# Row maxima transposed before they are clamped, bucket rows scaled on ACT, low parts subtracted on Pool

## The chip, the cores and the metric

The kernel runs on one core of a Trainium2 chip. The metric is the device time of one execution in microseconds (us). The engines are named as in the profile: PE (TensorE; PEld is its weight load), DVE (VectorE), ACT (ScalarE), POOL (GpSimd), SP (SyncE, which only issues transfers here). "SPq" and "ACTq" are the transfer queues of SP and ACT.

## The reference

Attention with buckets, and then a feed-forward net with a rational activation. There are 4 batches, 8 heads, 768 positions and 64 channels a head.

```python
q_bits = (np.einsum('bhsd,dk->bhsk', q, proj) > 0)          # 6 bits: the bucket of a position
mask = q_bucket[:, :, :, None] == k_bucket[:, :, None, :]
scores = np.where(mask, scale * (q @ k.T), -1e9)
scores = scores - np.max(scores, axis=-1, keepdims=True)
attn = np.exp(scores)
attn = attn / (np.sum(attn, axis=-1, keepdims=True) + 1e-09)
x = attn @ v                                                # -> 3072 tokens x 512
h = x @ w_in                                                # 512 x 2048
P = a0 + a1*h + a2*h**2 + a3*h**3
Q = 1 + |b0|*|h| + |b1|*h**2
out = (P / (Q + 1e-6)) @ w_out                              # 2048 x 512
```

## The kernel before

Two heads form a pair p, and there are 16 pairs. All large products run with float32 operands split in a rounded high part (fp32r) and the rest, the low part. For each pair:

- `high` rounds q and k on ACT into Q1 and K1 (tiles of 3 buffers); `high_move` brings half of them to the other partitions with two transfers; `low` subtracts the high part from the raw operand (DVE) into LO, of which there is one buffer for q and one for k; `second_low` and `second_high` send LO and Q1/K1 to Q2 and K2.
- `bits`, once for two pairs, projects q and k on 6 directions (PE, tile psb in PSUM), and DVE compares them with zero and subtracts a constant of the partition (tile mb); a second DVE operation multiplies each row by a factor of its partition, 2^60 or 1. `maskrows` moves the rows to rows 64 and up of Q1 and K1, so that a product over 76 rows gives the score plus a term of that size where bits differ.
- `maxstep(p, j)`, 12 times a pair, forms scores for 128 queries and 768 keys (PE, tile psm, two buffers) and reduces them to a column of M with a maximum (DVE).
- `shift_clamp` turns M (128 x 12) into nm = -max(M, -2^40) on DVE, SBUF to SBUF; `shift_turn` transposes nm on PE into PSUM (tile pst, one of the three "s" buffers, which scores use too) and copies it to mt on ACT; `shift_rows` moves mt to row 76 of Q1, where it shifts the scores.
- `scores(p, s)`, 12 steps a pair: the products pss on PE with keys on the partitions, exp on ACT into one of six E tiles, and additions of E tiles (acc, POOL), 8 a pair.
- `values` multiplies E with V (psv), `sums` adds up acc over the keys (psu), `values_out` and `sums_store` send both to DRAM; `recips` forms reciprocals on DVE once for 4 pairs.

`weights(i)`, 32 pieces spread over the attention, splits w_in and w_out in high and low parts (ACT, DVE): its DVE operations appear as wr, ws, wi_lo in the profile.

The order is written out by hand. `at(p, s, f, ...)` puts a step at place 12 p + s of a plan, sorted at the end; steps of the same place keep the order in which they were added. Each engine runs its instructions strictly in that program order (`Ordered`). Work for pair p is put two pairs ahead (`high`, `low`, `bits`, `maskrows`, `maxstep` from place 7 on) or one pair ahead (`second_low`, `second_high`, `load_v`, the shift steps at places 7, 8 and 10). Nearly all transfers are issued by SP. For pair 0 the shift is done in two halves of the queries (hf = 0, 1), and the steps ahead of the plan are written in line; the low parts of pair 1 are subtracted on Pool there.

The feed-forward net (`Ffn`, `Gemm1`: psh, pso, gl, c, w in the profile) follows, with PE as its busiest engine.

All instructions carry the line of the helper that issues them, L61; so groups are told apart by the names of tiles.

Of the kernel before, what the change touches and what calls it, by code (L numbers as in the profile page):

```python
# [7 lines left out]
F32 = mybir.dt.float32  # L8
# [3 lines left out]
AF = mybir.ActivationFunctionType  # L12
ALU = mybir.AluOpType
# [4 lines left out]
P = 128  # L18
S = 768
HQ = 384  # L20
NT = S // P
# [13 lines left out]
CLAMP = 2.0 ** 40  # L35
# [30 lines left out]
def move(nc, out, in_, queue=None):  # L66

    (queue or nc.sync).dma_start(out.bitcast(F32), in_.bitcast(F32))
# [3 lines left out]
def bucket_attention_then_rational_ffn(ctx, tc, qT, kT, v, proj, w_in, w_out, coef, consts, out):  # L72
# [55 lines left out]
    def operands_to_terms():  # L128
        early.close()
        ffn.terms_pool(right)  # L130

    last = attention(tc, nc, raw, ps_b, tail, tokens, early, operands_to_terms, ffn, load, QF, KF, v, w_in, w_out, wo_d, ident, cst,
                     ones, prj, wi_hi, wi_lo, x_d, s_d, r_d, coefficients)
    ffn.rest(ctx, last)
# [3 lines left out]
def attention(ctx, tc, nc, raw, ps_b, tail, tokens, early, operands_to_terms, ffn, load, QF, KF, v, w_in, w_out, wo_d, ident, cst, ones, prj,  # L138
# [9 lines left out]
    sm = ctx.enter_context(tc.tile_pool(name="sm", bufs=1))  # L148
# [5 lines left out]
    Q1, Q2, K1, K2, LO, V, M, MB, ACC, EXP, AV, MS = ({} for _ in range(12))  # L154

    def load_v(p, queue=nc.sync):
        V[p] = operand("v", p, [P, NT, P], F32)
        queue.dma_start(V[p], v[p])
# [3 lines left out]
    def high(p, t):  # L162
        F, T, n = ((QF, Q1, "q"), (KF, K1, "k"))[t]
        T[p] = operand(f"{n}1", p, [P, 2, S], F32R, 3)
        nc.scalar.copy(T[p][:, t, :], F[p])

    def high_move(p):
        for T, g in ((Q1[p], 0), (K1[p], 1)):
            move(nc, T[0:64, 1 - g, :], T[64:128, g, :])

    def low(p, t, engine=nc.vector):
        F, T = ((QF, Q1), (KF, K1))[t]
        LO[p, t] = raw.tile([P, S], F32R, tag=f"lo{t}", name=f"lo{t}_{p}", bufs=1)
        engine.tensor_tensor(out=LO[p, t], in0=F[p], in1=T[p][:, t, :].bitcast(F32), op=ALU.subtract)
# [13 lines left out]
    def bits(p, which=(0, 1)):  # L188

        if which[0] == 0:  # L190
            mb = sm.tile([P, 2, HQ], F32R, tag="mb", name=f"mb{p}")
            MB[p], MB[p + 1] = (mb, 0), (mb, 64)
        mb = MB[p + which[0]][0]
        sl = slice(64 * which[0], 64 * which[-1] + 64)
        ps = ps_a.tile([P, 2, 512], F32, tag="psa", name=f"psb{p}_{which[0]}")
        for hf in range(2):
            for w in which:
                for t, F in enumerate((QF[p + w], KF[p + w])):
                    o = 64 * w + 32 * t
                    nc.tensor.matmul(ps[o : o + 32, hf, 0:HQ], prj[:, t, :], F[:, hf * HQ : hf * HQ + HQ], start=True, stop=True)  # L200
        rows = mb[sl]
        nc.vector.tensor_scalar(out=rows, in0=ps[sl, :, 0:HQ], scalar1=0.0, scalar2=cst[sl, 0:1], op0=ALU.is_gt, op1=ALU.subtract)
        nc.vector.tensor_scalar(out=rows, in0=rows.bitcast(F32), scalar1=cst[sl, 1:2], scalar2=None, op0=ALU.mult)

    def maskrows(p, queues=(None, None)):
        mb, o = MB.pop(p)
        for h in range(2):
            o1 = o + 14 * h
            move(nc, Q1[p][64:76, h, :], mb[o1 : o1 + 12].rearrange("p f c -> p (f c)"), queues[0])
            move(nc, K1[p][64:77, h, :], mb[o1 + 32 : o1 + 45].rearrange("p f c -> p (f c)"), queues[1])  # L210
# [9 lines left out]
        nc.vector.tensor_reduce(out=M[p][:, j : j + 1], in_=ps[:, :, 0:HQ], axis=AX.XY, op=ALU.max)  # L220


    def shift_clamp(p, hf=None):
        m = M[p].rearrange("p (h f i) -> p h f i", h=2, f=2)
        m = m if hf is None else m[:, :, hf : hf + 1, :]
        n = NT if hf is not None else 2 * NT
        MS[p] = sm.tile([P, n], F32, tag="nm", name=f"nm{p}_{hf}")
        nc.vector.tensor_scalar(out=MS[p].rearrange("p (h f i) -> p h f i", h=2, i=NT // 2), in0=m, scalar1=-CLAMP, scalar2=-1.0,
                                op0=ALU.max, op1=ALU.mult)

    def shift_turn(p, hf=None):
        n = NT if hf is not None else 2 * NT
        ps = ps_b.tile([P, 512], F32, tag="s", bufs=3, name=f"pst{p}_{hf}")
        nc.tensor.transpose(ps[0:n, 0:P], MS.pop(p), ident)
        MS[p] = sm.tile([n, P], F32R, tag="mt", name=f"mt{p}_{hf}")
        nc.scalar.copy(MS[p], ps[0:n, 0:P])

    def shift_rows(p, hf=None):
        cs = slice(0, S) if hf is None else slice(hf * HQ, hf * HQ + HQ)
# [62 lines left out]
    def recips(bb):  # L302
        n = 2 * NHP * S // P
        s = tail.tile([P, n], F32, tag="rs", name=f"rs{bb}")
        nc.sync.dma_start(s, s_d[bb].rearrange("h (x c) -> (h x) c", c=n))
        yield
        z = tail.tile([P, n], F32, tag="rz", name=f"rz{bb}")
        d = tail.tile([P, n], F32, tag="rd", name=f"rd{bb}")
        r = tail.tile([P, n], F32, tag="rr", name=f"rr{bb}")
        nc.vector.tensor_scalar(out=z, in0=s, scalar1=0.0, scalar2=S * TINY, op0=ALU.is_equal, op1=ALU.mult)  # L310
        nc.vector.tensor_scalar(out=d, in0=s, scalar1=0.0, scalar2=1e-9, op0=ALU.is_gt, op1=ALU.mult)
        nc.vector.tensor_tensor(out=d, in0=s, in1=d, op=ALU.add)
        nc.vector.tensor_tensor(out=d, in0=d, in1=z, op=ALU.add)
        nc.vector.reciprocal(out=r, in_=d)
        yield
        nc.sync.dma_start(r_d[bb].rearrange("h (x c) -> (h x) c", c=n), r)
        yield
# [43 lines left out]
    def at(p, s, f, *args):  # L361
        plan.setdefault(12 * p + s, []).append((f, args))

    def spread(p, steps, gen):
        for s in steps:
            at(p, s, lambda g: next(g, None), gen)

    for p in range(NPAIR):
        for s in range(12):
            at(p, s, scores, p, s)  # L370

            if p > 1:
                at(p - 2, 7 + s if p > 2 else 9 + 0.85 * s, maxstep, p, s)

            if not 0 < p < NPAIR - 1:
                at(p, s + 2.3, values, p, s)
            elif s % 2:
                at(p, s + 1.3, values, p, s - 1)
                at(p, s + 1.3, values, p, s)
            if s % NT == NT - 1:  # L380
                at(p, s + (1.3 if 0 < p < NPAIR - 1 else 2.3), values_out, p, s // NT)
        for hf in range(2):
            at(p, 6 * hf + 9, values_store, p, hf)
        if p < NPAIR - 1:
            at(p, 14.5, sums, p)
            at(p, 16, sums_store, p)
        if p > 1:
            for t in range(2):
                at(p - 2, t, high, p, t)
                at(p - 2, 2 + t, low, p, t)  # L390
            if p % 2 == 0:
                at(p - 2, 3 if p == 2 else 2, bits, p)
            at(p - 2, 2, high_move, p)
            at(p - 2, 6 if p == 2 else 4, maskrows, p)
        if p > 0:
            at(p - 1, 0, second_low, p)
            at(p - 1, 3, second_high, p)
            at(p - 1, 4, load_v, p)
            d = 1.5 if p == 1 else 0
            at(p - 1, 7 + d, shift_clamp, p)  # L400
            at(p - 1, 8 + d, shift_turn, p)
            at(p - 1, 10 if d == 0 else 9.6, shift_rows, p)
        if p > 3:
            at(p - 4, 6, load, p)
        if p % NHP == NHP - 1 and p + 1 < NPAIR:
            spread(p, (20, 22, 23), recips(p // NHP))
# [12 lines left out]
    for t in range(2):  # L419
        high(0, t)  # L420
        low(0, t)
    bits(0, (0,))
    high_move(0)
    maskrows(0, (nc.sync, nc.scalar))
    load(2, nc.scalar)
    load_v(0, nc.scalar)
    bits(0, (1,))
    for t in range(2):
        high(1, t)
    second_low(0)  # L430
# [5 lines left out]
        at(-2, when[s], maxstep, 0, order[s])  # L436
        at(0, 0.6 + 0.7 * s, maxstep, 1, s)
    for hf in range(2):
        for s, f in ((5, shift_clamp), (6.5, shift_turn), (6.6, shift_rows)):
            at(-2, 19.5 * hf + s, f, 0, hf)  # L440
    for t in range(2):
        low(1, t, nc.gpsimd)
# [211 lines left out]
```

## Time and profile before

| | |
|---|---|
| median of 3 runs | 1029.55 us (1029.2 to 1035.9) |
| profiled execution | 1029.27 us, of which the span is 1027.5 us |
| busy PE | 977.0 us, 95% of the span |
| busy DVE | 907.9 us, 88% |
| busy ACT | 678.9 us, 66% |
| busy POOL | 384.8 us, 37% |
| transfers | 112.95 MB, mean 110 GB/s |

A row of a group reads: line, engine, operation, out<-in, shapes, count | busy us, mean ns of one | idle time of the engine just before, and what ended it. A row of waits reads: who waited <- for whom: us in total, times, longest. A row of the timeline reads: start us, length us, engine, operation, and in brackets the idle time before it and its releaser. The chain is the work that ended last, followed back from the end. A row of stretches gives the length and the busy time (instructions) of PE, PEld, DVE, ACT and POOL, the clock that PE was granted (1.00 is full speed), the busy share of the transfer engines and GB/s. A row of one tile gives min/median/max in ns.

### The profile page before, as it was taken

The page shows a single profiled execution, that of the slowest core. Times are in us where ns is not written, and L with a number is a line of the kernel's source. Part 1 is how long each engine was busy: PE and PEld are TensorE (multiplying, and loading weights), DVE is VectorE, ACT ScalarE, POOL GpSimd, SP SyncE. Part 2 cuts the span into 40 slices and gives each one's busy share as a digit, 9 for nine tenths or more (in the row PEclk, how much of TensorE's full clock was granted, in tenths as well). Part 3 has the DMA queues.
Part 4 walks back from the last instruction along what each step waited for, and adds up shares of the span by engine and source line. Part 5 has one row for each costly group of instructions (what it writes and reads, how often), then busy time and mean ns, then how long its engine had stood idle before and what let it go on. Part 6 is the DMA issues. An engine that isn't in the chain of part 4 may idle for free.

```text
span 1027.5 us, 14486 instructions
## 1 busy us (share of the span) xinstructions
PE 977.0 (95%) x5009; PEld 749.4 (73%) x5009; DVE 907.9 (88%) x1207; ACT 678.9 (66%) x1419; POOL 384.8 (37%) x268
## 2 busy tenths in 40 slices
PE   6899988989898988999999999999999999999998
PEld 2565555555555555564999999999999999999996
DVE  5688788878978787767999999999999999999996
ACT  1466555656656655567877777777777777777775
POOL 1255554545545454556222222222222222222222
PEclk7799999999999999899999999999999999999999
DMA  7765564656656664673740201101111010020000
GB/s 202 195 165 175 165 177 124 177 163 186 187 165 211 206 205 134 177 217 118 283 137 15 69 11 62 32 1 62 32 57 36 1 62 31 1 72 22 32 1 31
DMA packets 50489, 112.95 MB, mean 110 GB/s; under 512 B 9296, under 2 KB 21968, under 8 KB 50416
## 3 DMA queue, kind: packets, MB, share of 16 engines
q1 hardware_dynamic: 49580, 110.59, 35.8%
q10 hardware_dynamic: 836, 1.44, 0.5%
q8 instruction: 39, 0.64, 0.3%
q14 instruction: 34, 0.28, 0.1%
HBM read 56.82 MB, written 21.17 MB: 76 GB/s over the span
## 4 chain that ended last, share of the span: by engine, by line
PE 78%; DVE 13%; DMA 3%; issue 2%; ACT 2%; SPq 1%; DVEq 0%; ACTq 0%
PE psh L61 26%; PE pso L61 26%; PE psv L61 10%; PE pss L61 9%; PE psm L61 4%; DVE m L61 3%; DVE wr L61 2%; DVE ws L61 2%; DVE nm_None L61 2%; PE psu L61 2%; DVE wi_lo L61 2%; ACT E L61 1%; DMA k<-k 1%; PE psb L61 1%; SPq L61 1%
## 5 line engine op out<-in xcount | busy, mean ns | idle before, releaser
L61 POOL TENSOR_TENSOR gl<-c,gh 128x384 fp32r<-128x384 f32 x128 | 140.6, 1099 | 396.0 <-ACT gh L61 369.4
L61 DVE TENSOR_REDUCE m<-psm 128x1 f32<-128x768 f32 x192 | 180.1, 949 | 76.8 <-PE psm L61 76.2
L61 PE MATMUL pso<-wo,gh 128*128 128x512 f32 x768 | 241.1, 395 | 0.0
L61 ACT ACTIVATE E<-pss 128x384 f32<-128x384 f32 x384 | 168.4, 490 | 97.9 <-PE pss L61 92.4
L61 POOL TENSOR_TENSOR acc<-E,E 128x768 f32<-128x768 f32 x64 | 126.2, 1972 | 190.3 <-ACT E L61 190.3
L61 PE MATMUL pss<-q,k 77*128 77x384 f32 (+1 forms) x768 | 183.1, 361 | 3.0 <-DMA q<-mt 2.6
L61 PEld LDWEIGHTS pss<-q,k 77*128 77x128 f32 (+1 forms) x768 | 136.7, 196 | 64.6 <-issue 54.4
L61 PE MATMUL psh<-xl,wi_hi 128*128 128x384 f32 x512 | 172.1, 336 | 0.0
L61 PE MATMUL psh<-xh,wi_hi 128*128 128x384 f32 x512 | 171.7, 335 | 0.0
L61 PE MATMUL psh<-xh,wi_lo 128*128 128x384 f32 x512 | 171.5, 335 | 0.0
L61 PEld LDWEIGHTS pso<-wo,gh 128*128 128x128 f32 x768 | 142.9, 188 | 23.7
L61 PE MATMUL psv<-E,v 128*64 128x385 f32 x768 | 157.3, 529 | 0.0
L61 PE MATMUL pso<-wo,gl 128*128 128x512 f32 x384 | 152.2, 396 | 0.3 <-POOL gl L61 0.3
L61 DVE SCALAR_TENSOR_TENSOR c<-c,ab,r 128x384 f32<-128x384 f32 x128 | 147.1, 1149 | 0.0
L61 ACT ACTIVATE h<-psh 128x384 f32<-128x384 f32 x128 | 63.1, 493 | 122.4 <-PE psh L61 122.4
L61 POOL TENSOR_TENSOR acc<-acc,E 128x768 f32<-128x768 f32 x64 | 113.9, 1780 | 30.1 <-ACT E L61 27.5
L61 PE MATMUL psm<-k,q 76*128 76x384 f32 x384 | 111.1, 374 | 13.9 <-DVE m L61 9.8
L61 PEld LDWEIGHTS psh<-xh,wi_hi 128*128 128x128 f32 x512 | 96.1, 188 | 6.3 <-issue 1.2
L61 PEld LDWEIGHTS psh<-xl,wi_hi 128*128 128x128 f32 x512 | 96.0, 188 | 5.1
L61 PEld LDWEIGHTS psh<-xh,wi_lo 128*128 128x128 f32 x512 | 96.1, 188 | 0.0
L61 PEld LDWEIGHTS psm<-k,q 76*128 76x128 f32 x384 | 71.7, 204 | 31.8 <-DVE m L61 22.2
L61 PEld LDWEIGHTS psv<-E,v 128*64 128x64 f32 x768 | 47.6, 141 | 64.1 <-issue 56.7
(63 smaller groups left out, 1322.6 us busy)
## 6 DMA issues: line engine op xcount, KB each, us to landing
q<-q SPq DMA_DIRECT2D x48, 192.0 KB
k<-k SPq DMA_DIRECT2D x48, 192.0 KB
wr<-w_in SPq DMA_DIRECT2D x16, 512.0 KB
wr<-w_out SPq DMA_DIRECT2D x16, 512.0 KB
wo_d<-wr SPq DMA_DIRECT2D x16, 512.0 KB
wo<-wo_d SPq DMA_DIRECT2D x16, 512.0 KB
q<-lo SPq DMA_DIRECT2D x32, 192.0 KB
k<-lo SPq DMA_DIRECT2D x32, 192.0 KB
```

Source lines behind the costliest of these rows:

```text
L61: return self.tc.keep_in_program_order(issue(*args, **kwargs))
```

## The change

- `shift_clamp` is gone. `shift_turn` transposes M itself, and DVE clamps the result as it copies it out of PSUM to mt; ACT's copy is gone. For the two halves of pair 0 a DVE copy gathers the half's columns first.
- The scaling of the bucket rows becomes a step of its own, `penalties`, on ACT, one place behind `bits`.
- `low` runs on Pool for pairs 2 to 15.

```diff
--- before.py
+++ after.py
@@ -198,9 +198,12 @@
                 for t, F in enumerate((QF[p + w], KF[p + w])):
                     o = 64 * w + 32 * t
                     nc.tensor.matmul(ps[o : o + 32, hf, 0:HQ], prj[:, t, :], F[:, hf * HQ : hf * HQ + HQ], start=True, stop=True)
-        rows = mb[sl]
-        nc.vector.tensor_scalar(out=rows, in0=ps[sl, :, 0:HQ], scalar1=0.0, scalar2=cst[sl, 0:1], op0=ALU.is_gt, op1=ALU.subtract)
-        nc.vector.tensor_scalar(out=rows, in0=rows.bitcast(F32), scalar1=cst[sl, 1:2], scalar2=None, op0=ALU.mult)
+        nc.vector.tensor_scalar(out=mb[sl], in0=ps[sl, :, 0:HQ], scalar1=0.0, scalar2=cst[sl, 0:1], op0=ALU.is_gt, op1=ALU.subtract)
+
+    def penalties(p, which=(0, 1)):
+        sl = slice(64 * which[0], 64 * which[-1] + 64)
+        rows = MB[p + which[0]][0][sl]
+        nc.scalar.activation(rows, rows.bitcast(F32), AF.Identity, scale=cst[sl, 1:2])
 
     def maskrows(p, queues=(None, None)):
         mb, o = MB.pop(p)
@@ -220,20 +223,15 @@
         nc.vector.tensor_reduce(out=M[p][:, j : j + 1], in_=ps[:, :, 0:HQ], axis=AX.XY, op=ALU.max)
 
 
-    def shift_clamp(p, hf=None):
-        m = M[p].rearrange("p (h f i) -> p h f i", h=2, f=2)
-        m = m if hf is None else m[:, :, hf : hf + 1, :]
-        n = NT if hf is not None else 2 * NT
-        MS[p] = sm.tile([P, n], F32, tag="nm", name=f"nm{p}_{hf}")
-        nc.vector.tensor_scalar(out=MS[p].rearrange("p (h f i) -> p h f i", h=2, i=NT // 2), in0=m, scalar1=-CLAMP, scalar2=-1.0,
-                                op0=ALU.max, op1=ALU.mult)
-
     def shift_turn(p, hf=None):
-        n = NT if hf is not None else 2 * NT
+        n, m = 2 * NT, M[p]
+        if hf is not None:
+            n, m = NT, sm.tile([P, NT], F32, tag="nm", name=f"nm{p}_{hf}")
+            nc.vector.tensor_copy(m.rearrange("p (h i) -> p h i", h=2), M[p].rearrange("p (h f i) -> p h f i", h=2, f=2)[:, :, hf, :])
         ps = ps_b.tile([P, 512], F32, tag="s", bufs=3, name=f"pst{p}_{hf}")
-        nc.tensor.transpose(ps[0:n, 0:P], MS.pop(p), ident)
+        nc.tensor.transpose(ps[0:n, 0:P], m, ident)
         MS[p] = sm.tile([n, P], F32R, tag="mt", name=f"mt{p}_{hf}")
-        nc.scalar.copy(MS[p], ps[0:n, 0:P])
+        nc.vector.tensor_scalar(out=MS[p], in0=ps[0:n, 0:P], scalar1=-CLAMP, scalar2=-1.0, op0=ALU.max, op1=ALU.mult)
 
     def shift_rows(p, hf=None):
         cs = slice(0, S) if hf is None else slice(hf * HQ, hf * HQ + HQ)
@@ -387,9 +385,10 @@
         if p > 1:
             for t in range(2):
                 at(p - 2, t, high, p, t)
-                at(p - 2, 2 + t, low, p, t)
+                at(p - 2, 2 + t, low, p, t, nc.gpsimd)
             if p % 2 == 0:
                 at(p - 2, 3 if p == 2 else 2, bits, p)
+                at(p - 2, 4 if p == 2 else 3, penalties, p)
             at(p - 2, 2, high_move, p)
             at(p - 2, 6 if p == 2 else 4, maskrows, p)
         if p > 0:
@@ -397,7 +396,6 @@
             at(p - 1, 3, second_high, p)
             at(p - 1, 4, load_v, p)
             d = 1.5 if p == 1 else 0
-            at(p - 1, 7 + d, shift_clamp, p)
             at(p - 1, 8 + d, shift_turn, p)
             at(p - 1, 10 if d == 0 else 9.6, shift_rows, p)
         if p > 3:
@@ -420,11 +418,13 @@
         high(0, t)
         low(0, t)
     bits(0, (0,))
+    penalties(0, (0,))
     high_move(0)
     maskrows(0, (nc.sync, nc.scalar))
     load(2, nc.scalar)
     load_v(0, nc.scalar)
     bits(0, (1,))
+    penalties(0, (1,))
     for t in range(2):
         high(1, t)
     second_low(0)
@@ -436,7 +436,7 @@
         at(-2, when[s], maxstep, 0, order[s])
         at(0, 0.6 + 0.7 * s, maxstep, 1, s)
     for hf in range(2):
-        for s, f in ((5, shift_clamp), (6.5, shift_turn), (6.6, shift_rows)):
+        for s, f in ((6.5, shift_turn), (6.6, shift_rows)):
             at(-2, 19.5 * hf + s, f, 0, hf)
     for t in range(2):
         low(1, t, nc.gpsimd)
```

## Prediction

> **What bounds the kernel now.** I read the page first (the span and the chain that ended last), then the busy time by stretch, then PE's waits.
>
> ```profile
> span 1027.5 us, 14486 instructions
> ...
> PE psh L61 26%; PE pso L61 26%; PE psv L61 10%; PE pss L61 9%; PE psm L61 4%; DVE m L61 3%; DVE wr L61 2%; DVE ws L61 2%; DVE nm_None L61 2%; PE psu L61 2%; DVE wi_lo L61 2%; ACT E L61 1%; DMA k<-k 1%; PE psb L61 1%; SPq L61 1%
> ```
> ```profile
> 50.00:475.00 425.00, 390.64 (x2132) 238.82 (x2132) 348.49 (x361) 255.35 (x568) 225.04 (x120) 0.96 0.60 177
> 475.00:1027.50 552.50, 548.50 (x2751) 489.15 (x2749) 528.62 (x810) 409.38 (x826) 148.70 (x132) 1.00 0.15 51
> ```
>
> Two stages. The psh and pso products (half of the chain) fill the last stretch; there (columns: length, busy PE, weight load, DVE, ACT, POOL, granted clock) PE is busy 548.50 of 552.50 us at clock 1.00. The change doesn't touch them. The attention is the other stage. In its steady part, 50 to 475 us, PE idles 425.00 - 390.64 = 34.36 us and its clock averages 0.96. The change acts there and in the first 50 us. DVE holds 348.49 of the 425 us, but what matters is where PE waits for it:
>
> ```profile
> PE pst_None L61 <- DVE nm_None L61: 23.4, 13, 1.9
> ...
> PE psm L61 <- DVE m L61: 9.0, 15, 0.8
> ```
>
> In this stretch (total us, times, longest), 23.4 + 9.0 = 32.4 of the 34.36 idle us end with DVE. The largest is the transpose of the maxima waiting for its clamp `nm`. Why so long, for 12 columns?
>
> ```profile
> 193.06 1.95 POOL L61 TENSOR_TENSOR acc<-E,E 128x768 f32<-128x768 f32 x1 [2.94 <-ACT E L61]
> 193.26 1.78 DVE L61 TENSOR_SCALAR nm_None<-m 128x12 f32<-128x12 f32 x1
> ...
> 195.19 0.27 PE L61 MATMUL pst_None<-cst,nm_None 128*12 128x128 f32 x1 [1.84 <-DVE nm_None L61]
> ```
> ```profile
> L61 DVE TENSOR_SCALAR nm_None<-m x15: 160/1775/1779, 53.8 to 454.7; 128x12 f32<-128x12 f32 x15
> L61 DVE TENSOR_SCALAR mb<-psb,cst x9: 1004/1006/1023, 8.9 to 383.4; 128x768 fp32r<-128x768 f32 x7, 64x768 fp32r<-64x768 f32 x2
> ```
>
> The clamp needs 160 ns when undisturbed (min/median/max), and a median of 1775 ns. At 193.26 it starts inside Pool's 193.06 to 195.01 addition and ends with it (195.04): a DVE operation from SBUF to SBUF stands until Pool's ends. An operation of the same kind that reads PSUM, `mb<-psb`, doesn't: its nine are 1004 to 1023 ns long, Pool busy or not.
>
> **The change, part by part.**
>
> *Clamp behind the transpose.* The step `shift_clamp` goes; PE transposes M itself. What is late next? The transpose then needs the last reduce of the pair and a free PSUM buffer. The rows of the next pair show when PE reaches it:
>
> ```profile
> 220.72 0.95 DVE L61 TENSOR_REDUCE m<-psm 128x1 f32<-128x768 f32 x1
> ...
> 221.03 0.52 PE L61 MATMUL psm<-k,q 76*128 76x384 f32 x2
> 221.03 0.86 ACT L61 ACTIVATE E<-pss 128x384 f32<-128x384 f32 x2
> ...
> 221.38 0.88 PE L61 MATMUL pss<-q,k 77*128 77x384 f32 x4
> ```
>
> PE is there at 222.26; the reduce has ended at 221.67 and the exponentials that free the buffer at 221.89. So nothing is late next: **-23.4 us**. The other bound: if DVE is no earlier and some other wait takes half, -12. The new clamp sits on DVE between two reduces of the next pair, behind it the rest of DVE's queue. It waits for the transpose, which PE runs straight ahead of the maxima that DVE would need next, so nobody is held. Its size (12x128 from PSUM) isn't in the trace: between the 0.16 us above and the 1.01 us of `mb<-psb` with six times the columns; I take 0.3, off PE's path. The move of the row to Q1 has some 9 us: it is issued at 195.78 and the next pair's scores begin at 204.83 (both below).
>
> *Low parts to Pool, scaling to ACT.*
>
> ```profile
> L61 DVE TENSOR_TENSOR lo<-qf,q 128x768 fp32r<-128x768 f32 x15 | 15.6, 1039 | 7.0 <-ACT q L61 4.1 <-DMA q<-mt 2.8
> L61 DVE TENSOR_TENSOR lo<-kf,k 128x768 fp32r<-128x768 f32 x15 | 14.2, 950 | 0.9 <-ACT k L61 0.9
> L61 ACT CAST q<-qf 128x768 fp32r<-128x768 f32 x16 | 13.3, 832 | 10.3 <-DMA k<-mb 8.1 <-DMA qf<-qT 2.2
> L61 DVE TENSOR_SCALAR mb<-mb,cst 128x768 fp32r<-128x768 f32 x7 | 6.6, 938 | 0.2
> L61 POOL TENSOR_TENSOR lo<-kf,k 128x768 fp32r<-128x768 f32 x1 | 1.8, 1813 | 3.9 <-DMA k<-lo 3.9
> ```
> ```profile
> 195.19:224.12 28.93, 26.16 (x154) 16.04 (x155) 24.89 (x26) 17.10 (x38) 15.14 (x9) 1.00 0.60 176
> 224.12:252.67 28.55, 26.15 (x137) 16.08 (x138) 22.90 (x24) 17.16 (x38) 15.10 (x9) 0.94 0.56 159
> ```
>
> Pairs 2 to 15 move, 14 x (1039 + 950) = 27.8 us off DVE and 28 x 1813 = 50.8 us onto Pool. In the pair from 195.19, DVE's 24.89 us lose 1.78 (clamp), 1.99 (low parts) and 0.94 (scaling) and gain 0.3: 20.5. Pool's 15.14 become 18.8. ACT gains 0.83 (a cast of that shape) in every second pair and loses a 12x128 copy in each: 17.7 at most. PE's own 26.16 stays the longest.
>
> Place counts more than sums. Steps 2 to 4 of the pair:
>
> ```profile
> 195.78 0.77 SPq L61 DMA_DIRECT2D q<-mt_None  x1
> ...
> 204.83 0.97 PE L61 MATMUL pss<-q,k 77*128 77x384 f32 x4
> ...
> 208.66 2.13 POOL L61 TENSOR_TENSOR acc<-acc,E 128x768 f32<-128x768 f32 x1 [0.24 <-ACT E L61]
> ...
> 212.59 1.88 ACT L61 ACTIVATE E<-pss 128x384 f32<-128x384 f32 x4
> ...
> 214.11 0.95 DVE L61 TENSOR_TENSOR lo<-kf,k 128x768 fp32r<-128x768 f32 x1
> 214.16 0.79 SPq L61 DMA_DIRECT2D q<-mb  x1
> ...
> 214.54 2.22 POOL L61 TENSOR_TENSOR acc<-E,E 128x768 f32<-128x768 f32 x1 [3.75 <-ACT E L61]
> ...
> 218.23 0.61 PE L61 MATMUL psm<-k,q 76*128 76x384 f32 x2 [0.55 <-DVE m L61]
> ```
>
> Pool's gap, 210.79 to 214.54, is 3.75 us; the two subtractions want 3.6. They fit unless the second waits for its cast or for the K1 move; then the additions behind it are 1 to 2 us late. Nobody misses those soon: an E buffer comes round after 6 of a pair's 12 steps, 28.7 / 2 = 14 us. On DVE the subtraction at 214.11, 0.95 us, stood two operations ahead of the reduce that PE missed by 0.55 us at 218.23. None of these psm waits (9.0 us) is over 0.8 us, and DVE gets 1.9 us (low part and scaling) back ahead of this one. I take **-6 us**, two thirds. Ends: -9, and +3 (a third more) if Pool's longer string holds DVE more often.
>
> The scaled mask rows: the new ACT operation stands between the exponentials of steps 3 and 4, the four at 212.59 (1.88 us), so the rows are ready near 213.5 + 0.83 = 214.4 against the issue at 214.16: SP stands 0.25 us longer, with the other mask rows and the loads of the next operands behind it, and the exponentials behind ACT's operation come 0.83 us later, in a stretch where PE's next scores are products behind. The maxima that need the rows start at 221.03, 6.9 us after that first of four issues. I take 0; if all of it is used up, 0.25 x 7 = 2 us.
>
> *Clock.*
>
> ```profile
> 106.61 1.71 DVE nm_None L61
> ...
> 109.48 2.60 PE psv L61 x8
> ...
> 114.36 1.45 PE psv L61 x8
> ...
> 434.48 2.23 PE psv L61 x8
> ```
>
> In the chain (start, length), behind the stall for `nm` the same eight psv products take 2.60 us instead of 1.45, and the pair from 224.12, which begins with that stall too, has clock 0.94. The chain has such a stretch behind eight of the thirteen stalls (109.48 the first, 434.48 in the last of them), and none that only a wait of 0.8 us or less precedes. At mean 0.96, (1 - 0.96) x 425 = 17 us are lost in all. With the long stalls gone I take **-13 us**; ends 0 and -17.
> [...]
>
> *First 50 us.*
>
> ```profile
> 9.93 0.61 DVE L61 TENSOR_SCALAR mb<-mb,cst 64x768 fp32r<-64x768 f32 x1
> ...
> 34.40 0.41 PE L61 MATMUL pst<-cst,nm 128*6 128x128 f32 x1
> ...
> 36.51 0.96 DVE L61 TENSOR_TENSOR lo<-qf,q 128x768 fp32r<-128x768 f32 x1 [2.84 <-DMA q<-mt]
> ```
>
> The first scaling, 0.61 us on the path to the first mask rows, becomes 0.83 on ACT plus a handover: +0.3. The second transpose (34.40) now waits for a copy queued behind a reduce, about +1. DVE no longer stands 2.84 us for the subtraction at 36.51. Together 0 +- 2; I take +1.
>
> **Sum**, against the profiled execution's 1029.27 us (1.8 more than its span; the median of the runs, 1029.55, is the same): -23.4 - 6 - 13 + 1 = -41.4, so **988**. A cross-check: without their waits these two pairs take 26.2 and (28.55 - 2.4 idle - 1.7 slow clock) 24.4 us, 25.3 on average, against 28.7; over 13 pairs that is 44.
>
> **Rivals.**
> *The stall moves to psm.* DVE's weight operations meet Pool too:
>
> ```profile
> L61 DVE SCALAR_TENSOR_TENSOR ws<-ws,wr x32: 672/1214/2167, 47.2 to 483.8; 128x512 int32<-128x512 int32 x32
> L61 DVE TENSOR_TENSOR wi_lo<-ws,wi_hi x16: 676/684/2334, 55.9 to 272.2; 128x512 fp32r<-128x512 f32 x16
> ```
>
> Pool would be busy without a gap in steps 1 to 5, just where these stand. If in each pair one more of them goes from about 0.68 to 2.2 us and PE pays, 13 x 1.5 = 20 us come back: 1008; half of it, 998. For it: DVE is busy 24.89 us of a pair's 28.93 now. Against: it loses 4.4 of them net, and waits of 2.2 to 2.3 us are among the rows already. Chance 0.18.
> [...]
> *The slow clock stays.* The other terms alone give 1029.3 - 28.4 = 1001. Chance 0.10.
> *Nothing to measure.* The transpose stalls for the last reduce as long as it did for the clamp: 1020 to 1029. The reduce's end at 221.67 speaks against it. Chance 0.04.
> *Slower: Pool becomes the bound.* Its queue is in order; if the second subtraction stands for the K1 move each time and locks stretch its neighbours, the exponentials of step 10 wait for an E buffer that an addition still reads. It decides once Pool needs more than the 28.7 us of a pair; at 30.5, 13 x 1.8 = 23 us and 1053. Pool's 18.8 and some 3 of locks are far from it: 0.04.
>
> **How the numbers follow.** 988 has 0.64 (980 to 997 by the ends of its terms); with the first two rivals up to 1008, 0.90 or so lies between **978 and 1008**, less the tails. A change of 1% is about what a measurement of this kernel can tell from none: faster by more, 0.64 + 0.18 + 0.10 = 0.92; within, 0.04; slower, 0.04.
>
> **What would show it.** Right: no PE wait for the transpose over 0.3 us; the clamp at 0.2 to 0.4 us from PSUM; PE's idle time between 50 us and the end of attention under 10 us and its clock 0.99; pairs of 25 to 26 us; the last stretch (psh and pso) begins some 41 us earlier. Wrong: PE waits for `m` above 0.8 us at steps 4 to 6, weight operations on DVE near 2.2 us, or slow psv products behind short waits.

## The result, and the profile after

The changed kernel takes 987.87 us (median of 4 runs, 987.26 to 988.89) against 1029.38 us; the ratio is 0.9583, 95% interval 0.9545 to 0.9622. The profiled execution took 987.26 us, 42.0 us less than that of before. Its page begins, and has as its chain:

```profile
span 985.5 us, 14501 instructions
...
PE psh L61 27%; PE pso L61 27%; PE pss L61 12%; PE psv L61 11%; PE psm L61 6%; DVE ws L61 3%; DVE m L61 3%; PE psu L61 2%; PE psb L61 1%; DMA q<-mt 1%; DVE wr L61 1%; ACT E L61 0%; DMA k<-lo 0%; DVE c L61 0%; DMA v<-v 0%
```

The clamp `nm`, 2% of the chain before, is gone from it; pss, psv and psm have larger shares, 12, 11 and 6%. The stretches (length, busy PE, weight load, DVE, ACT, POOL, granted clock), with the second stage cut 43 us earlier:

```profile
50.00:432.00 382.00, 373.20 (x2136) 234.45 (x2137) 306.79 (x332) 255.34 (x561) 264.98 (x146) 1.00 0.67 197
432.00:985.50 553.50, 549.51 (x2756) 489.71 (x2752) 529.59 (x810) 409.78 (x828) 149.37 (x133) 1.00 0.15 51
```

The second stage is as long as it was, to 1 us. In the first PE idles 8.8 us in place of 34.4, and its clock is 1.00 in place of 0.96. PE's remaining waits there (total us, times, longest):

```profile
PE pss L61 <- ACT E L61: 4.0, 5, 1.1
PE psm L61 <- DVE m L61: 2.8, 4, 0.8
...
PE psb L61 <- DVE m L61: 1.3, 6, 0.2
```

No wait of PE for the transpose's input is left there. One transpose in the timeline (start, length), and the groups of its tiles and of the low parts (min/median/max in ns):

```profile
156.83 0.86 PE L61 MATMUL pss<-q,k 77*128 77x384 f32 x4
157.28 0.94 DVE L61 TENSOR_REDUCE m<-psm 128x1 f32<-128x768 f32 x1
157.53 0.27 PE L61 MATMUL pst_None<-cst,m 128*12 128x128 f32 x1
...
158.15 0.27 DVE L61 TENSOR_SCALAR mt_None<-pst_None 12x128 fp32r<-12x128 f32 x1
```
```profile
L61 PE MATMUL pst_None<-cst,m x15: 269/271/275, 57.8 to 413.1; 128*12 128x128 f32 x15
L61 DVE TENSOR_SCALAR mt_None<-pst_None x15: 267/268/279, 58.1 to 413.4; 12x128 fp32r<-12x128 f32 x15
...
L61 POOL TENSOR_TENSOR lo<-qf,q x15: 1802/1825/1842, 17.0 to 379.7; 128x768 fp32r<-128x768 f32 x15
L61 POOL TENSOR_TENSOR lo<-kf,k x15: 1804/1825/2274, 23.1 to 381.6; 128x768 fp32r<-128x768 f32 x15
```

PE goes from pss straight to the transpose. The clamp starts 0.35 us after the transpose has ended, behind a reduce of the next pair, and PE doesn't wait for it. It never takes more than 279 ns, though Pool is busy 69% of this stage (264.98 of 382 us). The first and the last of the 15 transposes are the two marks by which the kernels below are compared: 57.8 and 413.1 here, 55.5 and 455.0 before. So the steady part got 44.2 us shorter and the start 2.3 us longer.

### The profile page after: what moved, and what is told of

Its sections match the earlier page's. It is cut to its first block, busy times and chain, and to the rows that moved or that the text cites. A ratio compares the mean times of both kernels' runs of the same rounds, so it can differ in the third digit from the quotient of the medians.

```text
span 985.5 us, 14501 instructions
## 1 busy us (share of the span) xinstructions
PE 957.3 (97%) x5009; PEld 744.1 (76%) x5009; DVE 862.2 (87%) x1172; ACT 680.9 (69%) x1411; POOL 429.0 (44%) x296
## 4 chain that ended last, share of the span: by engine, by line
PE 87%; DVE 7%; DMA 2%; issue 1%; ACT 1%; SPq 0%; ACTq 0%; DVEq 0%
PE psh L61 27%; PE pso L61 27%; PE pss L61 12%; PE psv L61 11%; PE psm L61 6%; DVE ws L61 3%; DVE m L61 3%; PE psu L61 2%; PE psb L61 1%; DMA q<-mt 1%; DVE wr L61 1%; ACT E L61 0%; DMA k<-lo 0%; DVE c L61 0%; DMA v<-v 0%
## 5 line engine op out<-in xcount | busy, mean ns | idle before, releaser
L61 PE MATMUL pss<-q,k 77*128 77x384 f32 (+1 forms) x768 | 179.9, 357 | 6.2 <-ACT E L61 4.0
L61 PEld LDWEIGHTS pss<-q,k 77*128 77x128 f32 (+1 forms) x768 | 133.8, 192 | 63.9 <-issue 47.1
L61 POOL TENSOR_TENSOR acc<-E,E 128x768 f32<-128x768 f32 x64 | 124.2, 1941 | 102.5 <-ACT E L61 102.5
L61 PE MATMUL psv<-E,v 128*64 128x385 f32 x768 | 148.3, 503 | 0.0
L61 POOL TENSOR_TENSOR acc<-acc,E 128x768 f32<-128x768 f32 x64 | 109.8, 1715 | 31.6 <-ACT E L61 28.6
L61 PE MATMUL psm<-k,q 76*128 76x384 f32 x384 | 107.2, 363 | 8.8 <-DMA k<-mb 4.6
```

Source lines behind the costliest of these rows:

```text
L61: return self.tc.keep_in_program_order(issue(*args, **kwargs))
```

## The experiments

Theory A is the prediction's: DVE operations that Pool's additions hold make PE wait, the clamp above all. Theory B is the rival that DVE was simply short of time. Each kernel ran beside the kernel before.

| kernel | median us | ratio, 95% interval | PE waits for the transpose, us (times) | PE waits of psm for DVE, us | clock, 50 to 475 us |
|---|---|---|---|---|---|
| clamp moved, alone | 994.03 | 0.9653, 0.9622 to 0.9684 | 0.2 (1) | 9.7 | 1.00 |
| low parts on Pool, alone | 1002.65 | 0.9729, 0.9705 to 0.9753 | 13.8 (6) | 3.2 | 0.98 |
| scaling on ACT, alone | 1007.87 | 0.9771, 0.9740 to 0.9801 | 12.3 (7) | 7.0 | 0.98 |
| clamp in another form | 995.40 | 0.9661, 0.9631 to 0.9691 | 3.2 (13) | 10.0 | 1.00 |

(Waits are those of the whole execution.)

**The clamp alone.** `shift_turn` and the plan as changed, the rest as before.

> Before, with the clamp moved behind the transpose and nothing else. Theory A (the clamp in front of the transpose is held by Pool's addition, and PE pays for it, with a slow clock behind): the 23.4 us of PE waits for the transpose and most of the 13 to 17 us of slow clock go, the 9 us of psm waits stay, the first 50 us cost 2 us more: 990 to 997 us. Theory B (DVE is short of time as a whole, and any us taken off it counts alike): the clamps are 20 of the 55 us of DVE work that the change takes off, so 20/55 of 42 us: 1014 us.

994 us: theory A's. Three of the four terms of the sum are there, the transpose's, the clock's and the start's (the first transpose stands at 58.8 us in place of 55.5), and psm's waits stay at 9.7 us. Theory B would have had 1014.

**The clamp in front, but in a form that isn't held.** This one asks what holds it.

```diff
-            M[p] = sm.tile([P, 2 * NT], F32, ...)
+            M[p] = sm.tile([P, 3, 5], F32, ...)          # column j at [j // 4, j % 4]
-        nc.vector.tensor_scalar(out=MS[p]..., in0=m, scalar1=-CLAMP, scalar2=-1.0, op0=ALU.max, op1=ALU.mult)
+        nc.vector.tensor_scalar(out=MS[p].rearrange("p (a b) -> p a b", a=3), in0=M[p][:, :, 0:4], ...)
```

> Before, with the clamp in front of the transpose as it was and in the same place of DVE's queue, but M for pairs 1 to 15 laid out as 3 rows of 4 columns with a gap of one, so that the clamp reads 3 rows and writes one run of 12. [...] If the reading of SBUF itself is held, whatever the form, the clamps stay at 1.78 us and the time at 1029 us. Theory B: as for the moved clamp, 1014 us.

Its tile and PE's waits:

```profile
L61 DVE TENSOR_SCALAR nm_None<-m x15: 150/153/166, 54.4 to 421.2; 128x12 f32<-128x12 f32 x15
```
```profile
PE pst_None L61 <- DVE nm_None L61: 3.2, 13, 0.4
```
```profile
184.98 1.97 POOL L61 TENSOR_TENSOR acc<-E,E 128x768 f32<-128x768 f32 x1 [2.94 <-ACT E L61]
185.18 0.15 DVE L61 TENSOR_SCALAR nm_None<-m 128x12 f32<-128x12 f32 x1
```

The same data from the same memory, in the same place of the queue, and Pool is adding as before: 14 of the 15 clamps start inside an addition, most of them 0.2 us behind its start, just as the clamp at 193.26 did in the kernel before. They take 150 to 166 ns where the contiguous form took up to 1779. So the form of the operation decides here whether it is held, not the reading of SBUF by itself. What in the form decides, the gap in what it reads or the 3 rows, no run shows. The 13 waits of about 0.25 us that stay are the clamp's own length and handover, with the order unchanged; they cost no clock (1.00). For a form that isn't held I had expected about 0.2 us each, stalls under 0.4 us and 986 to 995 us: the longest stall is 0.4 us, and the time, 995.40 us, is 0.4 us above that band.

**The low parts alone, the scaling alone.**

> Before, with the low parts of pairs 2 to 15 on Pool and nothing else. Theory A: what counts is whether the clamp starts inside a Pool addition; DVE is earlier by up to 2 us in each pair, so some clamps start ahead of the addition and cost 0.16 us; between 988 (all of them) and 1024 us (none, only psm waits shorter), and the number of clamps of 1.78 us says which. Theory B: 28 of 55 us, so 1008 us, whatever the clamps do.

> Before, with the scaling of the bucket rows on ACT and nothing else. Theory A: DVE stood idle 2 us behind that operation, so nothing is gained: 1028 to 1030 us, and the clamp stalls stay at 23 us. Theory B: 7 of 55 us, so 1024 us.

The first lies between theory A's ends: six stalls are left. But only one of the six has a held clamp (1.77 us); in the other five the clamp takes 0.16 us, and what delays it comes below, with the clamp put back in front. The second contradicts what I expected: nothing but the scaling was taken off DVE, at a place where DVE stood idle behind it, and 23 us went. The timeline of such a pair shows how; the first line is from the kernel before (its addition, 214.54 to 216.76, stands in the prediction), the others are from the kernel with the scaling on ACT:

```profile
214.98 2.33 DVE L61 TENSOR_TENSOR wi_lo<-ws,wi_hi 128x512 fp32r<-128x512 f32 x1
```
```profile
208.09 0.94 ACT L61 ACTIVATE mb<-mb,cst 128x768 fp32r<-128x768 f32 x1
...
209.71 0.69 DVE L61 TENSOR_TENSOR wi_lo<-ws,wi_hi 128x512 fp32r<-128x512 f32 x1
209.86 2.25 POOL L61 TENSOR_TENSOR acc<-E,E 128x768 f32<-128x768 f32 x1 [4.18 <-ACT E L61]
...
215.88 0.16 DVE L61 TENSOR_SCALAR nm_None<-m 128x12 f32<-128x12 f32 x1
215.90 1.83 POOL L61 TENSOR_TENSOR acc<-E,E 128x768 f32<-128x768 f32 x1 [1.96 <-ACT E L61]
```

ACT's new operation holds up the exponentials behind it by 0.94 us, so Pool's addition starts at 209.86, 0.15 us after DVE's subtraction of the weights; before it was the other way round, 0.44 us behind the addition's start, and that subtraction took 2.33 us in place of 0.69. Six us later the clamp gets in 0.02 us ahead of the next addition and takes 0.16 us. If this is right, the work taken off DVE has no part in it, and useless work on ACT must do the same:

```diff
+    def extra(p):
+        spare = sm.tile([P, HQ], F32R, tag="spare", ...)
+        for hf in range(2):
+            nc.scalar.activation(spare, MB[p][0][:, hf, :].bitcast(F32), AF.Identity, scale=cst[:, 1:2])
...
+                at(p - 2, 4 if p == 2 else 3, extra, p)
```

> Before, all of DVE's work in its place, with useless ACT work in every second pair, two ACT operations of together about 1 us at the place where the change puts the scaling; they write to a spare tile. It tells why the scaling alone gave 23 us. Theory of order (the scaling on ACT holds up the exponentials of step 4 by 0.9 us, so Pool's addition there starts after DVE's subtraction of the weights instead of before it; that saves 1.65 us of DVE, and the clamp 6 us later gets in ahead of the next addition): the same happens here, the weights' subtractions of 2.3 us become half as many, about half of the clamps are 0.16 us, and the time is 1003 to 1014 us. Theory of work (0.94 us less on DVE is what counts): nothing is gained, 1028 to 1031 us.

It does: 1006.32 us, ratio 0.9781 (0.9746 to 0.9816), with 14 useless operations of 616 ns on ACT and all of DVE's work in place. Of the 16 weight subtractions wi_lo, 3 take 2.33 us in place of 7, and of the 15 clamps 8 are held in place of 14:

```profile
L61 DVE TENSOR_SCALAR nm_None<-m x15: 159/899/1781, 52.8 to 429.8; 128x12 f32<-128x12 f32 x15
```

Theory B falls with it. Which of two operations comes first decided nearly half of the stalls (7 of 13 are left): six clamps now start within 0.05 us of Pool's addition.

**Each part taken back from the changed kernel.**

> The changed kernel with the low parts back on DVE. If the parts mostly remove the same stall, this stays near the changed kernel: 988 to 993 us, with psm waits near 8 us and no waits for exponentials that DVE's weight operations make late (those came with Pool's longer work). If each part gives by the DVE work it takes off, 1010 us.

> The changed kernel with the scaling back on DVE. With no clamp in front of the transpose to be held, the order of the subtraction and the addition matters only for psm waits: 986 to 991 us. By DVE work, 993 us.

> The changed kernel with the clamp back in front of the transpose. Low parts on Pool left 6 clamps held and scaling on ACT 7; if these are different pairs, both together leave 0 to 3 and the time is 985 to 993 us, with the first 50 us 2 us shorter than in the changed kernel; if they are the same pairs, 998 to 1003 us.

| kernel | median us | ratio, 95% interval | PE waits for the transpose, us (times) | PE waits of psm for DVE, us |
|---|---|---|---|---|
| low parts back on DVE | 989.28 | 0.9609, 0.9587 to 0.9631 | 0.2 (1) | 7.1 |
| scaling back on DVE | 987.18 | 0.9593, 0.9561 to 0.9626 | none | 3.0 |
| clamp back in front | 1002.29 | 0.9746, 0.9707 to 0.9785 | 13.7 (6) | 4.2 |

Taken back last, the scaling is worth nothing that can be measured, and the low parts some 1.4 us by the medians (the intervals overlap). That isn't because neither does anything: against the clamp alone, 994.03 us, the low parts bring 7 us and the scaling 5 by the medians (their intervals just overlap with its own), and both together no more than can be told from either. For the low parts the waits show why: they take 3.4 us off psm's waits (7.1 us without them, 3.7 with them in the whole execution) and add 3.6 us of waits of pss for exponentials (0.4 and 4.0). With the clamp back in front both together are no better than the low parts alone: again six pairs stall, so the time lies in the second band. But the reason given there, that the two parts leave the same clamps held, isn't it. In none of the six is the clamp itself held:

```profile
126.12 1.81 POOL L61 TENSOR_TENSOR acc<-E,E 128x768 f32<-128x768 f32 x1 [1.29 <-ACT E L61]
126.17 2.30 DVE L61 CUSTOM_DVE_ANT_0 ws<-wr,ws 128x1024 uint16<-128x1024 uint16 x1
128.40 0.16 DVE L61 TENSOR_SCALAR nm_None<-m 128x12 f32<-128x12 f32 x1
...
128.71 0.27 PE L61 MATMUL pst_None<-cst,nm_None 128*12 128x128 f32 x1 [2.30 <-DVE nm_None L61]
```

DVE, now earlier, meets the same addition one operation sooner: the weight operation in front of the clamp is held and takes 2.30 us (0.67 in this place before), and the clamp stands behind it. Five of the six stalls with the low parts alone are of this kind. Moving the clamp takes both away from PE.

**Where the held operation goes then.** In the changed kernel the same weight operation is held in the same place, and shows up at PE through ACT:

```profile
130.27 1.82 POOL L61 TENSOR_TENSOR acc<-E,E 128x768 f32<-128x768 f32 x1 [1.31 <-ACT E L61]
130.30 2.34 DVE L61 CUSTOM_DVE_ANT_0 ws<-wr,ws 128x1024 uint16<-128x1024 uint16 x1
...
132.67 0.62 ACT L61 CAST wi_hi<-ws 128x512 fp32r<-128x512 f32 x1 [2.48 <-DVE ws L61]
133.19 0.86 ACT L61 ACTIVATE E<-pss 128x384 f32<-128x384 f32 x2
...
133.73 1.00 PE L61 MATMUL pss<-q,k 77*128 77x384 f32 x4 [1.14 <-ACT E L61]
```
```profile
L61 DVE CUSTOM_DVE_ANT_0 ws<-wr,ws x32: 673/676/2336, 51.2 to 444.0; 128x1024 uint16<-128x1024 uint16 x32
```

ACT stands 2.48 us for it with the exponentials behind, and PE 1.14 us for a buffer. Four of these operations take 2.33 us or more, and four of the five waits of pss, 3.7 of the 4.0 us, come some 3.4 us after their starts. Before, and with the low parts back on DVE, none of the 32 takes over 693 ns, and the one wait of 0.4 us that is left is the fifth. And in the start, the copy that gathers half of M is held by an addition too, with the second half transpose behind it:

```profile
34.68 1.67 POOL L61 TENSOR_TENSOR acc<-acc,E 128x768 f32<-128x768 f32 x1 [0.15 <-DMA q<-lo]
...
35.56 0.82 DVE L61 COPY nm<-m 128x6 f32<-128x6 f32 x1
...
36.52 0.37 PE L61 MATMUL pst<-cst,nm 128*6 128x128 f32 x1 [1.88 <-DVE nm L61]
```

Two edits answer these, alone and together. The first keeps the clamps of pair 0's halves in front, as before; the second is:

```diff
-        late = (10.5, 12.5, 13.5, 14.5) if i < 2 * NFC - 1 else (10.5, 10.8, 11, 11.2)
+        late = (11.5, 12.5, 13.5, 14.5) if i < 2 * NFC - 1 else (10.5, 10.8, 11, 11.2)
```

> The changed kernel with the two half clamps of pair 0 in front of their transposes as before (the other pairs as changed). The changed kernel reached the first transpose of the steady part 2.3 us later than the kernel before; if the copies that the half transposes wait for are the reason, 985 to 986.5 us, and no PE wait for nm in the first 50 us. If it is the scaling on ACT, no change: 988 us.

> The changed kernel with ACT's rounding of the weights one step later (11.5 in place of 10.5), behind the exponentials that it held up. In the changed kernel ACT stood up to 2.5 us for a DVE weight operation that Pool held (2.34 us instead of 0.68), and PE waited 4.0 us in 5 places for the exponentials behind it. If that is their cause, these waits fall to 0.4 us and the time to 983.5 to 985.5 us; if DVE's lateness reaches PE another way, 987 to 988 us.

> The changed kernel with both edits, the first clamps of pair 0 as before and the rounding of the weights one step later. If the two are independent, 981.5 to 983.5 us.

| kernel | median us | ratio, 95% interval | first and last transpose, us | PE waits of pss for exponentials, us |
|---|---|---|---|---|
| first clamps as before | 987.31 | 0.9596, 0.9564 to 0.9627 | 56.1, 409.2 | 2.0 |
| rounding later | 986.55 | 0.9587, 0.9573 to 0.9602 | 58.8, 412.8 | 1.5 |
| both | 982.63 | 0.9548, 0.9534 to 0.9563 | 56.2, 409.2 | 0.8 |

The first edit takes 1.7 us off the start, and no PE wait over 0.3 us for nm is left there; its runs spread from 983.5 to 991.8 us, so its median shows nothing. The second takes the waits for exponentials from 4.0 to 1.5 us, less than I expected, and its time lies between the two bands that I gave. It also did more than was meant: none of the four weight operations is held any longer (1.14 us at most), so it shows that the four waits go with the held operations, and not by itself that ACT's rounding hands them on; a new wait of 1.1 us stands at another place. Together they give 982.63 us, below each alone in the same round of measuring (its interval doesn't meet that of the later rounding, and just misses that of the first clamps). It is the fastest kernel here; against the changed kernel, measured in another round, the intervals overlap, so its 5 us there are likely, not shown.

**The price of Pool's time.** For the rival that Pool's work holds DVE:

```diff
-        engine.tensor_tensor(out=LO[p, t], in0=F[p], in1=T[p][:, t, :].bitcast(F32), op=ALU.subtract)
+        for _ in range(2 if p > 1 else 1):
+            engine.tensor_tensor(out=LO[p, t], ...)
```

> The changed kernel with each of Pool's subtractions for pairs 2 to 15 done twice, with the same result, 3.65 us more of Pool per pair. It prices the rival that Pool's work holds DVE. Pool would be busy 22 to 23 of the 25 us of a pair. If Pool's time is free as long as it isn't the longest engine, 987 to 990 us; if each us of Pool holds DVE's weight operations or delays the additions that the exponentials wait for, 995 to 1030 us.

998.39 us, ratio 0.9692 (0.9673 to 0.9712), 10.5 us above the changed kernel and in the second band. Its stretch, and one of its two longest waits with a held operation ahead of it:

```profile
50.00:432.00 382.00, 368.17 (x2062) 229.22 (x2062) 302.55 (x324) 244.64 (x537) 317.57 (x168) 0.98 0.66 192
```
```profile
166.17 1.68 POOL L61 TENSOR_TENSOR acc<-acc,E 128x768 f32<-128x768 f32 x1
166.26 1.64 DVE L61 TENSOR_TENSOR rd<-rs,rd 128x48 f32<-128x48 f32 x1
...
169.50 1.01 PE L61 MATMUL psm<-k,q 76*128 76x384 f32 x2 [3.13 <-DVE m L61]
```

Pool is busy 83% of the stage and still not the longest engine, yet the second 51 us of subtractions cost a fifth of their length, while the first cost nothing on balance. PE's two longest waits, 3.1 and 3.2 us, stand behind the reciprocals, where one more operation is now held (`rd`, 1.64 us; in the changed kernel it takes 0.21), and slow psv products follow both; the clock is back at 0.98.

## Why the prediction was right, point by point

988 was forecast and 987.87 measured. The mechanism of the two large terms, the stall and the slow clock behind it, is what the runs show. That the sum came out this close is luck, for not all terms are as sized:

- **The transpose, -23.4:** as forecast. The waits are gone, PE goes straight on, and the new clamp takes 0.27 us (0.3 was taken from bounds of 0.16 and 1.01).
- **psm, -6:** 9.0 us became 2.8. Three of the four that are left follow the reciprocals, at 0.79 to 0.81 us each.
- **Clock, -13:** mis-sized, low. The clock is 1.00 to two places where 0.96 was, so nearly the whole 17 us came back: PE's busy time, for the same 5009 products over the whole execution, fell from 977.0 to 957.3 us, by 19.7. That it hangs on the stalls is shown by the table: thirteen stalls of up to 1.9 us go with 0.96, six or seven with 0.98, none, or thirteen of at most 0.4 us, with 1.00. Stalls of 1.84 us were enough. Why some of them are followed by a slow stretch and others are not stays open: no run shows what sets the clock. That it might stay slow without the stalls (chance 0.10) was an estimate of mine; with the clamp moved alone, where 0.2 us of them is left, it is 1.00.
- **First 50 us, +1:** mis-sized; 2.3 us. The forecast had the copy queued behind a reduce (0.96 us), but not that the new copy is itself of the held kind (0.82 us in place of 0.17), nor that the first half's copy costs a wait too (3.1 us for both). Nor is the copy's kind all of it: in the kernel with the clamp moved alone the second copy takes 0.15 us and PE waits 3.6, because a held subtraction of the low parts stands ahead of it. What counts is the place in DVE's queue. All kernels with the first clamps in front have their first transpose at 53.7 to 56.2 us, those with the copies at 57.8 to 59.2.
- **The rival of Pool's longer string** was real in kind, with 0.68 to 2.3 us as priced, but it came out at another place than psm: through ACT at pss, 4.0 us against 0.4 before. Its sign, weight operations of 2.2 us or more in new places, came true for four of them. The prediction had followed DVE's held operations to PE by psm alone. The "some 3 of locks" that it adds to Pool's 18.8 us a pair, in the rival of Pool as the bound, is a term that no run shows. Before, an addition took 2.22 us with a subtraction of DVE still running at its start (214.54) and 1.83 us with only a reduce (236.98); after, Pool is busy 264.98 of 382 us, 17.6 us of a pair's 25.4.
- **Mask rows, 0:** one wait of 0.5 us for them in the steady part.

Sum with measured sizes: -23.4 - 6.2 - 17 + 3.6 + 0.5 + 2.3 = -40.2, against -42.0; the clock's second decimal alone is worth 0.005 x 425 = 2 us, and with PE's 19.7 us in place of the 17 it is -42.9. So a clock term that was too small by 4 to 7 us and costs that were left out or too small, 3.6 + 0.5 + 1.3 us, cancelled.

Where the reasoning was thin: it treated the parts as adding up, the low parts and the scaling as worth the psm waits. Alone they take away 28 and 23 us, mostly by moving the stalls of the clamp; with the clamp moved 7 and 5; and the second of the two adds at most 1.4 (all by the medians). The forecast for all three was right because the clamp's move takes away the stalls that the others would have taken, too, and because one of the others is enough for the rest.

## What to carry to other kernels

A tiny operation on a shared path deserves a look at its minimum and median: 160 against 1775 ns meant that it stood for another engine, and one that feeds PE should neither be of a kind that the trace shows held (the clamp, 1.78 us) nor queue behind one that is (the weight operation, 2.30 us). Gains of parts that remove the same stall don't add; a part that takes nothing off the path can still move the time by 2% (the useless work on ACT, ratio 0.9781), because it changes which operation comes first. A control that adds useless work in the same place tells the two apart.

## What the runs showed of the hardware that was not expected

- The same DVE operation on the same 12 columns is held by Pool as one run (up to 1779 ns) and not as 3 rows of 4 with a gap (at most 166 ns in 15).
- With a lead of 0.02 us over Pool's addition DVE's clamp ran at its own length, 0.16 us (at 215.88, with the scaling on ACT).
- In the steady part PE's clock fell behind stalls of 1.84 us and more, in some pairs and not in others, and in none of the kernels behind a wait of 1.2 us or less.
